# First units of an attention and mixer kernel: scores, state products and k transposes in the PSUM banks of token mixing, first state read from PSUM, order planned anew

## The chip, the core and the metric

The kernel runs on one core of a Trainium2 chip. The metric is the device time of one execution in microseconds (us); three executions of the kernel before took 617.54, 617.64 and 617.73. Engines are named as in the profile: PE (TensorE; PEld its weight loads), DVE (VectorE), ACT (ScalarE), POOL (GpSimd, here mostly a queue of transfers) and SP (SyncE, the other queue of transfers).

## What is computed

Four batches of 768 tokens, 8 heads of 48 (so 384 channels). A gated linear attention, then a mixer with complex phases over tokens and a channel product, then a gated unit with a second product over tokens:

```python
for t in range(S):
    state = alpha[:, :, t, :, None] * state + einsum('bhd,bhe->bhde', k[:, :, t], v[:, :, t])
    y[:, :, t] = einsum('bhd,bhde->bhe', q[:, :, t], state)
x = y as (B, S, 384)

theta = x @ w_theta
u = x + einsum('ts,bsd->btd', w_tok_r, x * cos(theta)) + einsum('ts,bsd->btd', w_tok_i, x * sin(theta))
x = u + maximum(u @ w_ch, 0)

h = maximum(x @ w_in, 0);  u, v = h[..., :512], h[..., 512:]
v_n = (v - mean(v)) / sqrt(var(v) + 1e-6)
v_s = einsum('ts,bsd->btd', w_spatial, v_n) + b_spatial[None, :, None]
out = (u * v_s) @ w_out
```

## The kernel before

Each batch is cut into six units of 128 tokens, 24 units u in all, each of two halves c of 64 tokens. A unit's path: its decay `al`, its `qk` and its `vd` are loaded by SP (`load_al`, `load_qk`, `load_v`). DVE scans the decay (`att_scan`, L485 to L489: a scan, a small reciprocal, a scan) and multiplies q and k with it (`att_qk`, L497). PE makes scores (`att_a`, L511, in the text also A), which DVE masks (`att_mask`, L519; one half is then moved to other partitions by SP, `move_a`), transposes k (`att_k`, L535, K), which ACT copies to `kt` (L539), and makes the state products `psu` of the two halves (`att_u`, L551, U). On DVE `att_t` (L566, L568) adds the decayed state to a product, into `tmp`, and `att_s` (L560) multiplies `tmp` with a decay into `ss`, the state that the next half reads. `att_y` (L585, Y) makes the unit's outputs `psy` from `ss`, q, masked scores and v; ACT copies them to `x` (L593). PE transposes x (`tr_p`, L605, P); ACT takes from it the upper part `xh` (`tr_h`, L609) and `xT`, DVE the rest (`tr_l`, L627). `th_p` (L637 with six matmuls, L640 with three, H) is the product with w_theta; ACT and DVE make r, sine and cosine and `z` from it (L644 to L666), and ACT and DVE split `z` in two parts `zs` (`z_h`, `z_l`, L670, L674). `tokmix(u, m, ri)` (L697, T) adds a unit's part of token mixing, six pieces of six matmuls a unit, into five PSUM banks acc0 to acc4 that stay with a batch until `evac`. Piece m = 0 writes acc0 and acc1, m = 1 acc1 and acc2, m = 2 acc3 and acc4; acc1 is zeroed ahead by DVE. After a batch, `ch_h` and `ch_l` split the result and `ch_p` (L739) multiplies it with w_ch into `psc`, which DVE adds (`ch_e`, L749). The second mixer (L812 to L920) follows for all batches.

PSUM has eight banks: five for acc, and three (`ps_tile`, tag `ps`) that all other results share: a `psa` for scores takes two of them, `psu` two, `psy` two, `psk`, `pst`, `th`, `psc` one each.

The weights come as 64-bit numbers in chunks, `raw`, by POOL's queue in two buffers. ACT takes part of a chunk into `zeros` (`top`, L382), DVE joins both into `wf` (`join`, L388), after which the buffer can be loaded again; ACT writes the upper part (`high`, L400) and DVE the lower (`low`, L408). The chunks are numbered: 0 and 1 w_theta (1 half as large), 2 to 13 the token weights of unit s and part ri (2 + 2s + ri; `in_w_tr` and `in_w_ti`), 14 and 15 w_ch.

The order of all steps on all engines is fixed when the program is built. Each step has an engine, an estimated cost, its predecessors and the buffers it needs; `latest` works out due times backwards, the tables OFF, OFF0, OFF3, UNIT and PIECE shift them per kind of step, batch, unit and chunk, and `order` plays the steps through in time and emits whichever is due first on an engine that is free. Each engine then works its steps strictly in that order, and so do the queues of SP and POOL.

Of the kernel before, what the change touches and what calls it, by code (L numbers as in the profile page):

```python
# [23 lines left out]
MAGIC = 12582912.0  # L24
# [26 lines left out]
    "cp": -158.47, "ce": 100.03, "cd": 447.07, "raw": -618.18, "bits": -49.65, "sgn": 1376.56, "mag": -710.85,  # L51
    "mul": 267.54, "high": -1464.25, "low": -859.94, "v": 16.07, "vr": 273.38, "vb": 866.6, "vw": 1642.18,
    "vm": -337.76, "vh": -1658.38, "vl": -557.55, "g_u": -7.44, "g_r": -485.14, "g_s": -429.06, "g_m": 441.16,
    "g_h": -488.08, "g_l": -904.44, "o_p": 15.51, "o_e": -843.47, "x2h": -1179.65, "x2l": 281.95, "x2": -552.71,
# [17 lines left out]
}  # L72
OFF3 = {
# [21 lines left out]
SSB = 6  # L95
# [6 lines left out]
ISSUE = {"dma": 0.4, "queue": 0.55}  # L102
AHEAD = {"dma": 0.8, "queue": 1.1}


# [180 lines left out]
def attention_mixer_kernel(  # L286
# [902 lines left out]
```

## Time and profile before

| | |
|---|---|
| median of three executions | 617.64 us |
| profiled execution, its own time | 613.52 us |
| its span, first to last instruction | 611.8 us |
| PE busy | 576.1 us, 94% |
| DVE busy | 399.2 us, 65% |
| ACT busy | 243.5 us, 40% |
| POOL busy | 24.8 us, 4% |

The profile is that of one execution. Busy time is the time in which at least one instruction of an engine runs. In a row of the trace the time in brackets is how long the engine stood idle before it, and for whom. The page cuts the span in forty slices of 15.3 us.

### The profile page before, as it was taken

The page shows a single profiled execution, that of the slowest core. Times are in us where ns is not written, and L with a number is a line of the kernel's source. Part 1 is how long each engine was busy: PE and PEld are TensorE (multiplying, and loading weights), DVE is VectorE, ACT ScalarE, POOL GpSimd, SP SyncE. Part 2 cuts the span into 40 slices and gives each one's busy share as a digit, 9 for nine tenths or more (in the row PEclk, how much of TensorE's full clock was granted, in tenths as well). Part 3 has the DMA queues.
Part 4 walks back from the last instruction along what each step waited for, and adds up shares of the span by engine and source line. Part 5 has one row for each costly group of instructions (what it writes and reads, how often), then busy time and mean ns, then how long its engine had stood idle before and what let it go on. Part 6 is the DMA issues. An engine that isn't in the chain of part 4 may idle for free.

```text
span 611.8 us, 13444 instructions
## 1 busy us (share of the span) xinstructions
PE 576.1 (94%) x5803; PEld 524.2 (86%) x5803; DVE 399.2 (65%) x671; ACT 243.5 (40%) x445; POOL 24.8 (4%) x45
## 2 busy tenths in 40 slices
PE   0688999999999999999999999999999999999997
PEld 0566878888888888888899889999999999999997
DVE  6898997986789796679855696544346434553060
ACT  2575665432534354233643543324233322242032
POOL 1101100000000000000000011000000000000000
PEclk9998999999999999999999999999999999999999
DMA  8667576333342423324023662200100010001002
GB/s 333 199 221 267 181 253 208 112 111 105 124 145 82 158 88 120 118 76 124 15 87 130 220 219 78 77 1 27 39 14 2 26 40 14 0 14 40 13 14 77
DMA packets 27370, 63.77 MB, mean 104 GB/s; under 512 B 2992, under 2 KB 12720, under 8 KB 26800
## 3 DMA queue, kind: packets, MB, share of 16 engines
q1 hardware_dynamic: 25136, 51.13, 24.9%
q0 software_dynamic: 2176, 11.80, 5.5%
q8 instruction: 45, 0.74, 0.5%
q14 instruction: 13, 0.11, 0.0%
HBM read 50.33 MB, written 9.44 MB: 98 GB/s over the span
## 4 chain that ended last, share of the span: by engine, by line
PE 73%; DVE 8%; DMA 4%; issue 2%; ACT 0%; SPq 0%; POOL 0%; DVEq 0%; ACTq 0%
PE acc L697 17%; PE sp L881 16%; PE po L910 8%; PE pu L865 8%; PE psv L823 8%; PE psc L739 4%; DMA al<-in_al 3%; PE th L637 3%; PE psy L585 3%; PE psu L551 1%; DVE al L485 1%; PE th L640 1%; PE psa L511 1%; DVE xT L711 1%; PE psk L535 1%
## 5 line engine op out<-in xcount | busy, mean ns | idle before, releaser
L697 PE MATMUL acc<-w,zs 128*128 128x512 f32 (+1 forms) x864 | 177.6, 347 | 0.3
L697 PEld LDWEIGHTS acc<-w,zs 128*128 128x128 f32 x864 | 134.8, 189 | 17.9 <-DVE zs L674 0.5
L881 PE MATMUL sp<-w,vns 128*128 128x384 f32 x576 | 105.6, 335 | 0.0
L881 PEld LDWEIGHTS sp<-w,vns 128*128 128x128 f32 x576 | 100.9, 188 | 0.7
L865 PE MATMUL pu<-xs,w 128*128 128x384 f32 x288 | 55.1, 336 | 0.0
L823 PE MATMUL psv<-w,xs 128*128 128x512 f32 x216 | 54.1, 395 | 0.0
L910 PE MATMUL po<-w,gs 128*128 128x384 f32 x288 | 53.2, 335 | 0.0
L865 PEld LDWEIGHTS pu<-xs,w 128*128 128x128 f32 x288 | 50.4, 188 | 0.8
L910 PEld LDWEIGHTS po<-w,gs 128*128 128x128 f32 x288 | 50.4, 188 | 0.5
L890 DVE TENSOR_TENSOR t<-sp,bsb 128x384 f32<-128x384 f32 x32 | 17.8, 557 | 50.7 <-PE sp L881 49.8
L823 PEld LDWEIGHTS psv<-w,xs 128*128 128x128 f32 x216 | 40.1, 187 | 7.8
L897 ACT CAST gs<-t 128x384 fp32r<-128x384 f32 x32 | 16.1, 514 | 74.4 <-DVE t L891 74.4
L739 PE MATMUL psc<-us,wch 128*128 128x384 f32 (+1 forms) x243 | 41.4, 321 | 1.7 <-DVE xT L749 1.1
L739 PEld LDWEIGHTS psc<-us,wch 128*128 128x128 f32 x243 | 37.8, 189 | 2.6 <-DVE xT L749 1.3
L901 DVE TENSOR_TENSOR gs<-t,gs 128x384 fp32r<-128x384 f32 x32 | 17.6, 556 | 30.8 <-ACT gs L897 30.7
L485 DVE TENSOR_TENSOR_SCAN al<-al,heads 112x536 f32<-112x536 f32 x24 | 30.5, 1271 | 7.9 <-DMA al<-in_al 7.8
L843 POOL TENSOR_TENSOR rs<-rs,mhalf 128x1 f32<-128x1 f32 x24 | 14.8, 618 | 460.7 <-DMA x<-x2d 275.1
L637 PE MATMUL th<-wth,xh 128*128 128x384 f32 x144 | 31.2, 352 | 1.7 <-DVE ax L519 1.0
L644 ACT ACTIVATE kk<-th,magic 128x384 f32<-128x384 f32 x24 | 13.9, 578 | 44.5 <-PE th L640 44.5
L489 DVE TENSOR_TENSOR_SCAN al<-al,heads 112x536 f32<-112x536 f32 x24 | 30.6, 1275 | 0.8
L535 PE MATMUL psk<-cst_sb,qk 112*128 112x112 f32 x96 | 14.0, 274 | 17.6 <-DVE qk L497 16.0
L497 DVE TENSOR_TENSOR qk<-qk,al 112x1024 f32<-112x1024 f32 x24 | 29.2, 1219 | 0.9 <-DMA qk<-in_qk 0.8
(77 smaller groups left out, 799.2 us busy)
## 6 DMA issues: line engine op xcount, KB each, us to landing
qk<-in_qk SPq DMA_DIRECT2D x24, 512.0 KB, 4.6
vd<-in_v SPq DMA_DIRECT2D x24, 288.0 KB, 4.1
al<-in_al SPq DMA_DIRECT2D x24, 268.0 KB, 2.7
raw<-in_w_ti POOLq DMA_DIRECT2D x6, 768.0 KB, 4.8
raw<-in_w_tr POOLq DMA_DIRECT2D x6, 768.0 KB, 5.9
x<-x2d SPq DMA_DIRECT2D x4, 1152.0 KB, 5.0
out<-o SPq DMA_DIRECT2D x24, 192.0 KB, 1.9
x2d<-xT SPq DMA_DIRECT2D x6, 576.0 KB, 3.3
```

Of the source, the lines that this page charges most:

```text
L485: nc.vector.tensor_tensor_scan(out=back[:, ::-1], data0=line[:, ::-1], data1=one[:, ::-1], initial=1.0, op0=ALU.mult, op1=ALU.add)
L489: nc.vector.tensor_tensor_scan(out=line, data0=line, data1=one, initial=0.0, op0=ALU.mult, op1=ALU.add)
L497: nc.vector.tensor_tensor(out=x, in0=x, in1=st[u]["ar"], op=ALU.mult)
L535: nc.tensor.transpose(psk[:, a, :], kh[:, a].rearrange("p c s -> p (c s)"), ident[:112, :112])
L585: nc.tensor.matmul(psy[par][64 * c:64 * c + 64, a, :], w, v, start=part == 0 or first, stop=part == 1,)
L637: nc.tensor.matmul(th, xh[:, 0, k], wth[:, pr, k], start=(k == 0 and pr == 0), stop=False)
L697: nc.tensor.matmul(acc[b, n][:, c0:c1], zs[:, pl, ri, m * 128:(m + 1) * 128], w[:, pr, t0:t1], start=first and n != 1, stop=last, skip_gro ...
L739: nc.tensor.matmul(ps, wch[:, pl, k, m * 128:(m + 1) * 128], us[:, pr, k], start=(n == 0), stop=(n == 3 * KD - 1),)
L823: nc.tensor.matmul(ps, xs2[:, pl, k, o:o + 128], win[pr, "v"][:, k], start=(n == 0), stop=(n == 3 * KD - 1),)
L865: nc.tensor.matmul(pu, win[f // 2][:, pl, k * 256 + f % 2 * 128:k * 256 + f % 2 * 128 + 128], xq[b, h][:, pr, k], start=(n == 0), stop=(n ...
L881: nc.tensor.matmul(sp[:, :TH], vns[b, s][:, pl, f * 128:(f + 1) * 128], wsp[s][:, pr, t], start=(n == 0), stop=(n == 3 * NS - 1),)
L910: nc.tensor.matmul(po, gs[b][:, pl, f, s * 128:(s + 1) * 128], wo[f // 2][:, pr, f % 2 * DM:(f % 2 + 1) * DM], start=(n == 0), stop=(n == ...
```

## The change

The function `unit_ps` gives the first EARLY units a bank of token mixing in place of a shared one: scores (`psa`) acc0 and acc2, state products (`psu`) acc3 and acc4, the k transpose (`psk`) acc3, for units 0 to 2. Outputs, x transposes and `th` stay with the three shared banks.

In the first unit of a batch, the first state product is no longer copied to `tmp`: `att_s(u, 1)` reads `psu` itself. (`att_i`, a matmul that would add a state in PSUM, and `th_n`, `th_m`, with which `r` would be made by PE, come into the text, but STP and THP are empty and `att_i` is for other units, so neither issues an instruction.) One more constant, `unmagic`, is set by DVE at the start. The ring of `ss` has five buffers instead of six.

The planner's costs of transfers are set a little higher, its engines start at times FIRST instead of 0, and all five tables have new numbers, so that the order differs throughout the program.

```diff
+EARLY = {'a': 3, 'u': 3, 'y': 0, 'k': 3, 't': 0, 'h': 0}
+BANKS = {'a': [0, 2], 'u': [3, 4], 'k': [3]}
+THP = ()
+STP = ()
-SSB = 6
+SSB = 5
-ISSUE = {"dma": 0.4, "queue": 0.55}
-AHEAD = {"dma": 0.8, "queue": 1.1}
+FIRST = {"pe": 0.8, "dve": 1.6, "act": 2.2, "pool": 1.5, "dma": 0.74, "none": 0.0, "queue": 1.5}
+ISSUE = {"dma": 0.44, "queue": 0.57}
+AHEAD = {"dma": 0.8, "queue": 1.0}
 PIECE = {
-    "0": -331.5, "1": -441.59, "2": -706.09, "3": -715.22, "4": -65.4, "5": -167.4, "6": 8.34, "7": 308.88,
+    "0": -679.06, "1": -1253.41, "2": -607.1, "3": -578.67, "4": -112.62, "5": -191.42, "6": 185.74, "7": -410.35,
...
+    def unit_ps(u, what, n, shape, name):
+        if u < EARLY[what]:
+            bank = f"acc{BANKS[what][n]}"
+            size = math.prod(shape[1:])
+            t = accp.tile([128, 512], F32, tag=bank, name=bank)[:, :size]
...
+        return ps_tile(shape, name)
...
-            st[u]["psa", e] = ps_tile([128, 2, 2, 64], "psa")
+            st[u]["psa", e] = unit_ps(u, "a", e, [128, 2, 2, 64], "psa")
-        psk = st[u]["psk"] = ps_tile([128, NP, 112], "psk")
+        psk = st[u]["psk"] = unit_ps(u, "k", 0, [128, NP, 112], "psk")
-            st[u]["psu", c] = ps_tile([128, NP, D], "psu")
+            st[u]["psu", c] = unit_ps(u, "u", c, [128, NP, D], "psu")
...
-        nc.vector.tensor_tensor(out=ss, in0=tmps.pop(0), in1=decay(u, c), op=ALU.mult)
+        tmp = st[u]["psu", 0][:112] if c and summed(u) else tmps.pop(0)
+        nc.vector.tensor_tensor(out=ss, in0=tmp, in1=decay(u, c), op=ALU.mult)
+
+    def summed(u):
+        return u % NS == 0 or u in STP
...
-        psu = st[u]["psu", c][:112]
-        if u % NS == 0 and c == 0:
-            nc.vector.tensor_copy(out=tmp, in_=psu)
-        else:
-            nc.vector.tensor_tensor(out=tmp, in0=psu, in1=st[u]["ss", c], op=ALU.add)
+        nc.vector.tensor_tensor(out=tmp, in0=st[u]["psu", c][:112], in1=st[u]["ss", c], op=ALU.add)
```

What the new tables do to the order is seen in the program's rows. Three places follow, with row by row what an engine does; line numbers of the new program are some 20 to 35 higher.

The first is DVE's start. `al` is the decay of a unit (101 is unit 0's; 105 before and 103 now are unit 1's), `wf` the joined chunk, `qk` the decayed q and k. Before:

```order
L485 SCALAR_TENSOR_TENSOR al_101<-al_101,heads_89 112x536
L488 RECIPROCAL al_101<-al_101 112x8
L489 SCALAR_TENSOR_TENSOR al_101<-al_101,heads_89 112x536
L388 SCALAR_TENSOR_TENSOR wf_122<-raw_103,zeros_92 128x768
L485 SCALAR_TENSOR_TENSOR al_105<-al_105,heads_89 112x536
L488 RECIPROCAL al_105<-al_105 112x8
L489 SCALAR_TENSOR_TENSOR al_105<-al_105,heads_89 112x536
L408 SCALAR_TENSOR_TENSOR w_127<-wf_122,w_127 128x768
L497 TENSOR_TENSOR qk_109<-qk_109,al_101 112x1024
```

And now:

```order
L506 SCALAR_TENSOR_TENSOR al_101<-al_101,heads_91 112x536
L509 RECIPROCAL al_101<-al_101 112x8
L510 SCALAR_TENSOR_TENSOR al_101<-al_101,heads_91 112x536
L506 SCALAR_TENSOR_TENSOR al_103<-al_103,heads_91 112x536
L509 RECIPROCAL al_103<-al_103 112x8
L510 SCALAR_TENSOR_TENSOR al_103<-al_103,heads_91 112x536
L409 SCALAR_TENSOR_TENSOR wf_129<-raw_105,zeros_94 128x768
L518 TENSOR_TENSOR qk_114<-qk_114,al_101 112x1024
L429 SCALAR_TENSOR_TENSOR w_131<-wf_129,w_131 128x768
```

The scan of unit 1 moved ahead of the first chunk's `join`, and the first `att_qk` ahead of its `low`.

The second is ACT's start, from its second chunk on: `zeros` is the taking of a chunk, `w` and `wth` its `high`, then `kt`, `x`, `xh` and `xT` of units 0 and 1. Before (from the third `zeros` on):

```order
L382 ACTIVATE zeros<-raw 128x768
L539 COPY kt<-psk 128x448
L400 ACTIVATE w<-wf 128x768
L382 ACTIVATE zeros<-raw 128x384
L400 ACTIVATE wth<-wf 128x384
L539 COPY kt<-psk 128x448
L382 ACTIVATE zeros<-raw 128x768
L400 ACTIVATE wth<-wf 128x768
L382 ACTIVATE zeros<-raw 128x768
L593 COPY x<-psy 128x4x48 x2
L609 CAST xh<-pst 128x384
```

And now (from the second `zeros` on):

```order
L403 ACTIVATE zeros<-raw 128x384
L560 COPY kt<-acc_138 128x448
L421 ACTIVATE wth<-wf 128x384
L403 ACTIVATE zeros<-raw 128x768
L560 COPY kt<-acc_219 128x448
L421 ACTIVATE wth<-wf 128x768
L403 ACTIVATE zeros<-raw 128x768
L620 COPY x<-psy 128x4x48 x2
L421 ACTIVATE w<-wf 128x768
L403 ACTIVATE zeros<-raw 128x768
L636 CAST xh<-pst 128x384
```

The chunks of w_theta moved to the second and third place, `xh` of unit 0 now stands behind the fifth `zeros` (before, the sixth), with one `high` and one `zeros` between `x` and `xh`. POOL's queue loads in the same order of chunks: 13, 1, 0, 2, 3, 7 now, 13, 3, 2, 1, 0, 10 before. SP loads `al`, `al`, `vd`, `cst`, `qk` now, and loaded `al`, `al`, `qk`, `cst`, `qk`, `vd` before.

The third is DVE ahead of the first token mixing: `r` of unit 1 (L648, now L681), masks of unit 2, `qk` of units 2 and 3, `z` and `zs` of unit 0. Before:

```order
L497 TENSOR_TENSOR qk_314<-qk_314,al_266 112x1024
L497 TENSOR_TENSOR qk_378<-qk_378,al_307 112x1024
L666 TENSOR_TENSOR z_413<-z_413,x_316 128x768
L648 SCALAR_TENSOR_TENSOR r_450<-kk_427,th_405 128x384
L519 TENSOR_TENSOR ax_454<-psa_432,cst_sb_69 128x256
L519 TENSOR_TENSOR am_461<-psa_433,cst_sb_69 128x256
L388 SCALAR_TENSOR_TENSOR wf_467<-raw_275,zeros_92 128x768
L674 TENSOR_TENSOR zs_452<-z_413,zs_452 128x768
```

And now:

```order
L540 TENSOR_TENSOR ax_430<-acc0_397,cst_sb_69 128x256
L540 TENSOR_TENSOR am_432<-acc2_398,cst_sb_69 128x256
L506 SCALAR_TENSOR_TENSOR al_311<-al_311,heads_91 112x536
L509 RECIPROCAL al_311<-al_311 112x8
L510 SCALAR_TENSOR_TENSOR al_311<-al_311,heads_91 112x536
L681 SCALAR_TENSOR_TENSOR r_465<-kk_463,th_420 128x384
L518 TENSOR_TENSOR qk_366<-qk_366,al_311 112x1024
L700 TENSOR_TENSOR z_428<-z_428,x_291 128x768
L409 SCALAR_TENSOR_TENSOR wf_475<-raw_298,zeros_94 128x768
L595 TENSOR_TENSOR tmp_497<-acc3_441,ss_372 112x192
L708 TENSOR_TENSOR zs_495<-z_428,zs_495 128x768
```

The scan of unit 3 and `r` of unit 1 moved ahead of `att_qk(3)` and of unit 0's `z` and `zs`, and a state sum of unit 2 stands there too. On PE the steps up to the first token mixing were K0 A0 K1 A1 U0 U1 Y0 P0 Y1 H0 P1 H1 K2 A2 K3 A3 and are now K0 A0 U0 A1 K1 U1 Y0 P0 Y1 H0 P1 K2 A2, the first part of H1, U2, its second part, K3 A3; Y2 now stands behind the first piece, U3 behind the third.

## Rows read from the trace of the kernel before

**Rows 1.** Page, the span in forty slices: PE's busy tenths.

```profile
PE   0688999999999999999999999999999999999997
```

**Rows 2.** Windows: length, busy PE, PEld, DVE, ACT, POOL (instructions), granted clock, DMA.

```profile
3.44:85.98 82.54, 57.94 (x871) 48.70 (x872) 72.11 (x108) 45.42 (x76) 7.88 (x14) 0.98 0.71 248
15.63:80.74 65.11, 53.71 (x849) 45.01 (x850) 58.52 (x90) 41.14 (x70) 7.34 (x13) 0.97 0.67 228
...
30.00:40.00 10.00, 8.71 (x92) 7.43 (x92) 9.86 (x14) 6.77 (x14) 0.53 (x1) 1.00 0.92 326
...
50.00:60.00 10.00, 8.26 (x177) 6.82 (x181) 8.51 (x14) 6.10 (x10) 1.07 (x2) 0.83 0.74 252
80.74:340.00 259.26, 256.02 (x3482) 224.12 (x3477) 201.77 (x320) 111.71 (x216) 0.00 (x0) 1.00 0.36 118
```

**Rows 3.** Waits (us, times, longest): PE up to 61 us; DVE, 3.4 to 86.

```profile
PE psk L535 <- DVE qk L497: 16.0, 2, 15.6
PE psu L551 <- ACT kt L539: 3.0, 2, 2.3
...
PE psu L551 <- DVE ax L519: 1.4, 1, 1.4
PE psk L535 <- ACT kt L539: 1.1, 1, 1.1
...
DVE wf L388 <- ACT zeros L382: 5.8, 3, 3.6
...
DVE w L408 <- ACT w L400: 0.9, 1, 0.9
...
DVE wth L408 <- ACT wth L400: 0.6, 1, 0.6
```

**Rows 4.** Timeline of DVE from its first scan: start, duration, [idle before].

```profile
3.44 1.27 DVE L485 TENSOR_TENSOR_SCAN al<-al,heads 112x536 f32<-112x536 f32 x1 [1.08 <-DMA al<-in_al]
...
4.98 1.27 DVE L489 TENSOR_TENSOR_SCAN al<-al,heads 112x536 f32<-112x536 f32 x1
9.90 0.96 DVE L388 SCALAR_TENSOR_TENSOR wf<-raw,zeros 128x768 uint32<-128x768 uint32 x1 [3.64 <-ACT zeros L382]
...
14.36 1.22 DVE L497 TENSOR_TENSOR qk<-qk,al 112x1024 f32<-112x1024 f32 x1
```

**Rows 5.** DVE's groups, shapes apart: busy us, mean ns, idle before.

```profile
L560 DVE TENSOR_TENSOR ss<-tmp,al 112x192 f32<-112x192 f32 x44 | 15.6, 355 | 1.0
...
L566 DVE COPY tmp<-psu 112x192 f32<-112x192 f32 x4 | 1.4, 351 | 2.6 <-PE psu L551 2.6
```

**Rows 6.** Issues, us to landing: at 1.6-2.0 us, at 2.1-2.2, all (median).

```profile
qk<-in_qk SPq DMA_DIRECT2D x1, 512.0 KB, 6.8
...
raw<-in_w_ti POOLq DMA_DIRECT2D x1, 768.0 KB, 8.8
...
al<-in_al SPq DMA_DIRECT2D x24, 268.0 KB, 2.7
...
raw<-in_w_tr POOLq DMA_DIRECT2D x6, 768.0 KB, 5.9
```

**Rows 7.** Timeline of PE, single rows between 30 and 85 us.

```profile
32.98 2.29 PE L637 MATMUL th<-wth,xh 128*128 128x384 f32 x6
...
37.27 1.33 PE L637 MATMUL th<-wth,xh 128*128 128x384 f32 x6 [0.69 <-ACT xh L609]
...
43.26 1.74 PE L697 MATMUL acc<-w,zs 128*128 128x256 f32 x6
...
80.74 1.31 PE L697 MATMUL acc<-w,zs 128*128 128x256 f32 x6
...
83.06 1.28 PE L637 MATMUL th<-wth,xh 128*128 128x384 f32 x6 [1.01 <-DVE ax L519]
```

**Rows 8.** Timeline of DVE, the state product `att_s(5, 1)`.

```profile
85.63 0.35 DVE L560 TENSOR_TENSOR ss<-tmp,al 112x192 f32<-112x192 f32 x1
```

**Rows 9.** Waits of PE from 80.74 us to the end, the longest.

```profile
PE pst L605 <- DVE xT L749: 1.3, 1, 1.3
```

More of the change, by code (lines that the diff above doesn't have):

```diff
@@ L44 @@
 OFF = {
[6 rows of a table removed]
[L51 to L54, printed above, removed]
[6 rows of a table added]
+    "ce": -880.9, "cd": 1489.21, "raw": -473.63, "bits": -921.27, "sgn": 2210.86, "mag": 1308.55, "mul": 394.64,
+    "high": -1533.93, "low": -1460.32, "v": 143.66, "vr": -33.61, "vb": 570.25, "vw": 3214.81, "vm": 824.68,
+    "vh": -1464.39, "vl": 159.16, "g_u": 130.27, "g_r": -797.41, "g_s": -2037.89, "g_m": -595.78, "g_h": -2481.78,
+    "g_l": -415.04, "o_p": -583.54, "o_e": 982.08, "x2h": -1502.64, "x2l": 734.13, "x2": -883.6,
 }
@@ L167, in finish @@
                 push(when[f], "ready", f)
+    for e, t in free.items():
+        push(t, "tick", None)
     for k in keys:
@@ L312, in ps_tile @@
         return psp.tile(shape, F32, tag="ps", name=name)
+    def unit_ps(u, what, n, shape, name):
[3 more added lines that the diff above has]
+            t = accp.tile([128, 512], F32, tag=bank, name=bank)[:, :size]
+            if len(shape) == 2:
+                return t
+            sub = {f"d{i}": k for i, k in enumerate(shape[1:])}
+            return t.rearrange(f"p ({' '.join(sub)}) -> p {' '.join(sub)}", **sub)
+        return ps_tile(shape, name)
     cst_sb = const.tile([128, 192], F32, name="cst_sb")
@@ L318, in attention_mixer_kernel @@
     nc.vector.memset(magic, MAGIC)
+    unmagic = const.tile([128, 1], F32, name="unmagic")
+    nc.vector.memset(unmagic, -MAGIC)
     halfpi = const.tile([128, 1], F32, name="halfpi")
@@ L331, in attention_mixer_kernel @@
     minus = pb.tile([128, 128], F32R, name="minus") if XLP else None
+    negative = pb.tile([128, 128], F32, name="negative") if THP else None
     NB = 2
@@ L426, in conv @@
             c["queue"] = nc.gpsimd if n < NQ else nc.sync
-            k = step(early + OFF["raw"], "queue" if n < NQ else "dma", 2.1 * size, raw_f64, n, after=before, tiles=[raw])
+            k = step(early + OFF["raw"], "queue" if n < NQ else "dma", 2.2 * size, raw_f64, n, after=before, tiles=[raw])
             k = step(early + OFF["mag"], "act", cost(0.54, 0.86), top, n, after=[k], tiles=[raw, zero])
@@ L559, in att_s, with att_i @@
         ss = st[u]["ss", c] = pa.tile([112, NP, D], F32, tag="ss", name="ss", bufs=SSB)
[L560 removed]
+        tmp = st[u]["psu", 0][:112] if c and summed(u) else tmps.pop(0)
+        nc.vector.tensor_tensor(out=ss, in0=tmp, in1=decay(u, c), op=ALU.mult)
+    def summed(u):
+        return u % NS == 0 or u in STP
+    def att_i(u):
+        nc.tensor.matmul(
+            st[u]["psu", 0][:112].rearrange("p a e -> p (a e)"), ident[:112, :112],
+            st[u]["ss", 0].rearrange("p a e -> p (a e)"), start=False, stop=True, skip_group_check=True,
+        )
     def att_t(u, c):
         tmp = tmps[0] = pa.tile([112, NP, D], F32, tag="tmp", name="tmp", bufs=1)
[L564 to L568 removed]
+        nc.vector.tensor_tensor(out=tmp, in0=st[u]["psu", c][:112], in1=st[u]["ss", c], op=ALU.add)
     def att_y(u):
         qh, vd = st[u]["qh"], st[u]["vd"]
[L572 removed]
+        psy = st[u]["psy"] = [unit_ps(u, "y", n, [128, NP, D], "psy") for n in range(2)]
         for a in range(NP):
@@ L644, in th_k, with th_n, th_m @@
         nc.scalar.activation(kk, st[u]["th"], AF.Identity, bias=magic)
+    def th_n(u):
+        nc.scalar.activation(st[u]["kk"], st[u]["kk"], AF.Identity, bias=unmagic)
+    def th_m(u):
+        nc.tensor.matmul(st[u]["th"], negative, st[u]["kk"], start=False, stop=True, skip_group_check=True)
     def th_r(u):
@@ L661, in th_s @@
         else:
[L662 removed]
+            r, turn = (st[u]["th"], TURN) if u in THP else (st[u]["r"], -TURN)
+            nc.scalar.activation(z[:, 1], r, AF.Sin, scale=turn)
     def z_m(u):
@@ L926, in negate @@
     def negate():
-        nc.scalar.activation(minus, ident, AF.Identity, scale=-1.0)
+        for x in (minus, negative):
+            if x is not None:
+                nc.scalar.activation(x, ident, AF.Identity, scale=-1.0)
     step(0.0, "dma", 0.32, load_cst)
-    if XLP:
-        step(0.0, "act", 0.3, negate, after=[("load_cst",)])
+    if XLP or THP:
+        step(0.0, "act", 0.5, negate, after=[("load_cst",)])
     conv_small(w_theta, wth, "wth", scale=INV_2PI)
@@ L952, in attention_mixer_kernel, with ps @@
         xt = ("xT", 2, b)
-        def ps(*n):
-            return ("ps", 3, (u,) + n)
+        def ps(what, n=0):
+            if u < EARLY[what]:
+                return (f"acc{BANKS[what][n]}", 1, (u, what, n))
+            return ("ps", 3, (u, what, n))
         def at(name, eng, cost, fn, *args, after=(), tiles=(), by=None):
@@ L986, in attention_mixer_kernel @@
             if ss:
-                k = at(f"s{c}", "dve*", 0.27, att_s, c, after=[ksc, ktx], tiles=[al, *ss, *tmps_in])
+                k = at(f"s{c}", "dve" if c and mine else "dve*", 0.27, att_s, c, after=[ksc, ktx], tiles=[al, *ss, *tmps_in])
                 kss.append(k)
-            if not (final and c):
+            if c == 0 and mine:
+                ktx = at("t0", "pe", 0.33, att_i, after=[k, ku, ("load_cst",)], tiles=[ps("u", 0), *ss]) if i else ku
+            elif not (final and c):
                 ktx = at(f"t{c}", "dve", 0.27, att_t, c, after=[k, ku], tiles=[ps("u", c), ("tmp", 1, (u, c)), *ss])
```

33 lines of the change are left out of this document (18 added, 15 removed), and 35 rows, old and new, of tables (OFF, OFF0, OFF3).

## Prediction, made before the changed kernel ran

> **What bounds the kernel now.** I read the page's slices first: PE is full from the eighth of the forty slices on and not ahead of it [rows 1]. So there are two stretches. Cut up by windows, PE has 53.71 us of work in the 65.11 us from its first matmul at 15.63 to 80.74, and 256.02 in the 259.26 us from there to 340 [rows 2]. What can be won lies before about 80 us: 15.6 us in which PE has nothing yet, and 11.4 us (65.11 less 53.71) of holes behind that. Later, the longest single wait is 1.3 us [rows 9].
>
> The waits of PE up to 61 us name what the change is about [rows 3]. 15.6 us are for the first decayed k (`qk` from DVE). Of the holes two are PSUM: a k transpose that waits until ACT has read the one before (1.1), state products that wait until DVE has masked scores (1.4); these want buffers, not data. Others want data: `psu` waits for the transposed k (3.0, two waits, the longer 2.3).
>
> But who paces these 80 us? From its first scan at 3.44 up to the end of `att_s(5, 1)`, DVE works 72.11 of 82.54 us [rows 2, 8]. Whatever order PE has, it needs these DVE steps; so I count what the new order does to DVE's 10.4 us of idling, and then what PE makes of it.
>
> **The change part by part.** *Banks.* Units 0 to 2 take scores, state products and k transposes from the five accumulator banks, idle until token mixing starts. PE's work is the same instructions. It takes away the buffer waits above: 1.1 + 1.4 = 2.5 us of PE holes. On the path that sets the end it is worth nothing of its own as long as DVE (87% busy) is what PE catches up with; what it does is to let PE run its early work as soon as DVE has it. Where DVE is not the pace, these 2.5 us are the bound above. The banks add a wait: the first tokmix pieces of unit 0, at 43.26 in before [rows 7], must now follow unit 2's masks and state sums on DVE, since m = 2 writes acc3 and acc4; behind a waiting piece stand all of PE's later steps. DVE does these steps for the states of unit 2 anyway, so the price stays inside the DVE budget below.
>
> *First state.* The COPY of `psu` to `tmp` goes, four in all, 0.35 each [rows 5]; the decay multiply reads PSUM instead. One of the four lies in the paced stretch: -0.3 us. The other three stand where PE is full: 0. The bound from the other side is a multiply that is slower from PSUM; the COPY, which reads PSUM, and the multiply, which read SBUF, cost the same for the same shape (351 and 355 ns) [rows 5], so 0.
>
> *Order at the start.* Unit 1's scan now stands directly behind unit 0's, ahead of the first weight chunk (`wf`, `join`). In before DVE had nothing from 6.25 to 9.90: 3.64 us until ACT's `zeros` of that chunk [rows 4]. A scan step takes 3.44 to 6.25, 2.81 us, and fits, if the second `al` is there: both are the first that SP issues, and an `al` lands in 2.7 [rows 6]. So 0.83 us of the hole are left: **2.8 us won**. The first `att_qk` then follows the chunk, at 10.8 in place of 14.36, if `qk` has landed. In before it landed 6.8 us behind its issue at 1.7, so at 8.5 [rows 6]. Now `vd` and `cst` (288 + 96 KB) go ahead of it on SP, but POOL's second chunk is 384 KB instead of 768: two `al`, `qk`, two chunks before, or two `al`, `vd`, `cst`, `qk` and a chunk and a half now, are 2584 KB in either order. In before these had all landed when POOL's second chunk had, 8.8 us behind an issue that ran at 2.1 to 2.2: by 11.0 [rows 6]. So `qk` is there at 11.0 at the latest, `att_qk` takes 1.22 [rows 4], and PE's first matmul comes at about 12.2, 3.4 us earlier.
>
> *Order of chunks.* DVE waits 5.8 us in three waits for ACT's `zeros`, the longest 3.6: the other two make 2.2, or 1.1 each. It waits 0.9 and 0.6 us in `low` for ACT's `high` [rows 3]. The new order puts `att_qk`, masks or state steps between `join` and `low` of the first chunks, so I take these 1.5 as gone. Of the 2.2 I take half, 1.1: the chunks come earlier in the program, but one lands 5.9 us behind its issue [rows 6] and only two are in flight, as before; the bounds are 0 and 2.2. *New waits.* On ACT the cast `xh` of unit 0 stands behind the `zeros` of the fifth chunk (second place above), and POOL issues that chunk only when the third, the big one of theta, has been joined; in before it was the sixth, but PE was later still. Behind the cast wait `tr_l(0)` on DVE and `th_p(0, 0)` on PE. I take for it what a wait for such a chunk costs on the mean, -1.1; 0 if the chunk is early, 3.6, the longest of the three, if not. Unit 5's scan now stands close behind `att_s(3, 1)`, which frees its `al` buffer: 2.7 to land [rows 6], beside a `join` and a `low` of 0.9 each, as long as the `wf` of [rows 4]: -0.9. A third, of `r` of unit 1 for PE, is a rival below.
>
> *Sum.* 2.8 + 0.3 + 1.5 + 1.1 - 1.1 - 0.9 = 3.7 us less idling of DVE. PE has 27 us to give until 80.74 (15.6 and 11.4), so I take its gain as what DVE gives. To this comes one PE wait of that stretch that did not hang on DVE's pace but on order: 1.0 us at 83.06, where `th` wanted the PSUM buffer of scores that DVE had not masked yet [rows 7]. It had one tokmix piece between the scores of unit 5 and itself, now it has three; each lasts 1.3 [rows 7]. It goes: 0.8 to 1.0. Together **4.5 us**. The profiled execution took 613.5 (span 611.8 and 1.7 around it), so it would be 609.0; the median of the shown runs is 4.1 above that execution, and I take the saved time as the same there: 617.6 - 4.5 = 613.1. Behind 80 us the order changes everywhere too; the waits of PE there are few and none is longer than 1.3 [rows 9], so +-1.3 for one of them gone or come; with the chunk waits' bounds (+1.1, -1.1) this makes the forecast's own range 611.4 to 615.0.
>
> **The rivals.** *All holes go.* If both new waits vanish and the chunk waits too, DVE gains 2.8 + 0.3 + 1.5 + 2.2 = 6.8, with PE's 1.0 7.8; and a piece of PE's low clock may go as well: from 50 to 60 us, behind the wait of 2.3 us, the granted clock is 0.83 [rows 2, 3]. 8 us: 609.6. For it: PE gets its inputs in time for nearly all of unit 0 to 2. Against: it leaves DVE 3.6 of 10.4 us idle, 96% busy for 80 us.
>
> *The clock stays down.* Six `th` matmuls took 2.29 us at 32.98 and 1.33 at 37.27 [rows 7]. [...] In the new order (third place above) `r` of unit 1 stands on DVE ahead of `att_qk(3)`, `z_m(0)` and the `zs` that the first tokmix piece needs, and on PE U2 now stands between the two parts of `th_p(1)`, whose end `r` waits for. At the slow durations the first part is 1.0 longer, the second, with half the matmuls, 0.5, and for U2 I take 0.7, an estimate by its smaller matmuls: 2.2 us in which DVE waits. 4.5 - 2.2 = 2.3: 615.3.
>
> [...]
>
> *The banks decide nothing.* The change could do less than it says: if chunks arrive no earlier than before, DVE's steps behind them stay where they were, the head start ends as longer waits for `zeros` and `xh` (3.6, the longest seen [rows 3], in place of 1.1: 2.5 more), nothing of the 1.1 is won and 0.9 of the 1.5 in `low` comes back: 4.5 - 2.5 - 1.1 - 0.9 = 0: 617.6. For it: three of DVE's waits hang on chunks. Against: POOL issues a chunk when DVE has joined one, and DVE joins earlier.
>
> *Slower.* The pieces `psc` (ch_p) of the channel product (6 for each of three batches) now stand among other K, P and Y of the next batch than before, with three shared PSUM buffers, emptied by DVE. One such wait costs 1.3 us, at 236 us [rows 9]. It decides from the fifth of the eighteen on that waits so (5 x 1.3 = 6.5, against 4.5). Two in each of the three batches: 7.8 - 4.5, so 620.9. Against it: DVE has 22% idle from 80 to 340 [rows 2].
>
> **How the numbers follow.** Forecast 613.1: 0.55. All holes 609.6: 0.15. Clock 615.3: 0.14. Nothing 617.6: 0.09. Slower: 0.07. Two tenths of a per cent, 1.2 us, is about what a measurement can tell from no change: faster means under 616.4. Forecast, all holes and nearly all of the clock case lie there: 0.83; same 0.10; slower 0.07. The range has to hold 0.8: forecast, clock and most of the case of all holes, so from 609.0 to 616.4; what it leaves out are the last two cases and the tails.
>
> **What would show it.** First matmul at 12.2 (11.5 to 13); no 3.6 us hole on DVE before 10; no PSUM buffer wait of PE among units 0 to 2; `psk` and `psu` not behind ACT or masks; a wait of DVE `xh` of about 1 us near 26; first tokmix piece ahead of 43.26 by 3 us (by 1 if the clock stays down); DVE idle from its first scan to `att_s(5, 1)` of about 6.7 us, not 10.4; no wait of `th` for masks near 80. Wrong if the first matmul is early and unit 3's first tokmix piece, at 80.74 in before, is not, or if more than 2 us of new PE waits stand between 80 and 340.

## The result, and the profile after

The changed kernel took 609.96 us (median of four executions, 609.87 to 611.83) beside 617.59 for the kernel before (615.29 to 617.73): a ratio of 0.9892, 95% interval 0.9863 to 0.9922. The predicted 613.1 was 3.1 too high; the time lies inside the range of 609.0 to 616.4, near its lower end. Faster was the sign that came.

The profiled execution of the changed kernel took 610.03 us (span 608.3), that of the kernel before 613.52. So the two profiles differ by 3.5 us, and the medians by 7.6. Both numbers are needed below. One further execution of the changed kernel, in the last comparison, took 3131.63 us; its time is left out everywhere.

The page's slices of PE, to lay beside [rows 1]: in both kernels PE is full (9, that is 90% or more) from the fifth slice on. The four slices ahead of it read 1, 7, 7, 8 now and 0, 6, 8, 8 before.

```profile
PE   1778999999999999999999999999999999999997
```

To see where the 3.5 us lie, I cut both executions at the first `psv` of the second mixer, which is the same instruction in both and has the same 1451 matmuls behind it. Windows of the kernel before, and then of the changed one (length, busy PE, PEld, DVE, ACT, POOL with instructions, granted clock, DMA share, GB/s):

```profile
0.00:86.00 86.00, 57.96 (x872) 48.70 (x873) 73.34 (x114) 46.93 (x78) 10.00 (x21) 0.98 0.70 244
86.00:345.25 259.25, 257.02 (x3485) 225.00 (x3483) 197.94 (x312) 113.20 (x217) 0.00 (x0) 1.00 0.37 120
...
345.25:611.80 266.55, 261.14 (x1451) 250.53 (x1449) 127.96 (x246) 83.32 (x151) 14.82 (x24) 1.00 0.13 44
```

```profile
0.00:86.00 86.00, 63.47 (x993) 52.89 (x997) 74.94 (x118) 47.18 (x83) 9.50 (x20) 0.96 0.71 241
86.00:341.35 255.35, 252.37 (x3376) 221.03 (x3368) 197.98 (x309) 114.01 (x214) 0.53 (x1) 1.00 0.40 128
...
341.35:608.30 266.95, 262.90 (x1451) 252.33 (x1449) 124.38 (x243) 81.54 (x149) 15.11 (x24) 1.00 0.11 39
```

The first `psv` comes 3.9 us earlier (345.25 to 341.35). Up to there PE idles 25.5 us (341.35 less 63.47 and 252.37) in place of 30.3 (345.25 less 57.96 and 257.02): 4.8 us less, of which its matmuls, 0.9 us longer in sum, take some back. Behind it the changed kernel is 0.4 us longer: 1.4 us less idle, and 1.8 us more for the same 1451 matmuls.

Of the 4.8 us, 3.2 are the earlier first matmul (15.63 in before [rows 2], 12.43 now). Timelines of the changed kernel's start, on DVE and then on PE (start, duration, [idle before <- whom it waited for]); DVE's answer to [rows 4]:

```profile
4.99 1.27 DVE L510 TENSOR_TENSOR_SCAN al<-al,heads 112x536 f32<-112x536 f32 x1
6.18 1.25 DVE L506 TENSOR_TENSOR_SCAN al<-al,heads 112x536 f32<-112x536 f32 x1
...
10.05 0.96 DVE L409 SCALAR_TENSOR_TENSOR wf<-raw,zeros 128x768 uint32<-128x768 uint32 x1 [1.07 <-ACT zeros L403]
11.14 1.23 DVE L518 TENSOR_TENSOR qk<-qk,al 112x1024 f32<-112x1024 f32 x1
...
15.91 0.35 DVE L582 TENSOR_TENSOR ss<-acc,al 112x192 f32<-112x192 f32 x1
```

```profile
12.43 1.01 PE L556 MATMUL acc<-cst_sb,qk 112*128 112x112 f32 x4 [12.43 <-DVE qk L518]
```

The second scan fills the hole of 3.64 us, and 1.07 of it is left. The row at 15.91 is the multiply that now reads the state product in PSUM. The waits, to lay beside [rows 3]: PE up to 86 us (behind the one for the first `qk`), then DVE from 3.4 to 86.

```profile
...
PE psk L556 <- DVE qk L518: 3.2, 1, 3.2
PE pst L632 <- ACT x L620: 2.3, 2, 1.7
PE psy L612 <- DMA ay<-ax: 1.3, 1, 1.3
PE th L664 <- ACT x L620: 0.9, 1, 0.9
PE acc L572 <- ACT kt L560: 0.7, 1, 0.7
PE psk L556 <- DVE ax L540: 0.5, 1, 0.5
...
```

```profile
DVE al L506 <- DMA al<-in_al: 2.0, 2, 1.1
DVE wf L409 <- ACT zeros L403: 1.9, 2, 1.1
DVE xh L654 <- ACT xT L641: 1.5, 2, 1.3
DVE qk L518 <- DMA qk<-in_qk: 1.3, 1, 1.3
DVE wth L429 <- ACT wth L421: 0.9, 1, 0.9
DVE r L681 <- ACT kk L671: 0.9, 1, 0.9
DVE w L429 <- ACT w L421: 0.4, 1, 0.4
```

PE no longer waits for ACT's read of an earlier k transpose; one wait of 0.5 us for masks is left, at 81.13 us (`psk` of a later unit, one of the shared buffers). Both waits for chunks (`wf`) are shorter. The forecast's new wait for `xh` is there.

### The profile page after: what moved, and what is told of

Read it like the earlier page. It is cut to its first block, busy times and chain, and to the rows that moved or that the text cites. A ratio compares the mean times of both kernels' runs of the same rounds, so it can differ in the third digit from the quotient of the medians.

```text
span 608.3 us, 13440 instructions
## 1 busy us (share of the span) xinstructions
PE 578.7 (95%) x5803; PEld 526.3 (87%) x5803; DVE 397.3 (65%) x668; ACT 242.7 (40%) x445; POOL 25.1 (4%) x45
## 4 chain that ended last, share of the span: by engine, by line
PE 75%; DVE 10%; DMA 8%; issue 4%; ACT 2%; SPq 1%; DVEq 0%; ACTq 0%; POOLq 0%
PE acc L731 17%; PE sp L915 17%; PE psv L857 8%; PE pu L899 8%; PE po L944 8%; PE psc L773 6%; DMA qk<-in_qk 4%; PE psy L612 3%; PE th L664 3%; PE th L667 1%; DVE qk L518 1%; PE psu L572 1%; DMA al<-in_al 1%; PE psa L532 1%; DVE wf L409 1%
## 5 line engine op out<-in xcount | busy, mean ns | idle before, releaser
L731 PE MATMUL acc<-w,zs 128*128 128x512 f32 (+1 forms) x864 | 174.1, 347 | 1.5 <-DVE xT L745 0.8
L915 PE MATMUL sp<-w,vns 128*128 128x384 f32 x576 | 106.9, 338 | 0.0
L870 DVE BATCH_NORM_STATS2 stt<-v 128x6 f32<-128x512 f32 x24 | 16.6, 690 | 21.4 <-ACT v L865 21.2
L704 ACT CAST zs<-z 128x768 fp32r<-128x768 f32 x24 | 20.0, 834 | 24.0 <-DVE z L700 13.1
```

Of the source, the lines that this page charges most:

```text
L704: nc.scalar.copy(out=st[u]["zs"][:, 0], in_=st[u]["z"])
L731: nc.tensor.matmul(acc[b, n][:, c0:c1], zs[:, pl, ri, m * 128:(m + 1) * 128], w[:, pr, t0:t1], start=first and n != 1, stop=last, skip_gro ...
L915: nc.tensor.matmul(sp[:, :TH], vns[b, s][:, pl, f * 128:(f + 1) * 128], wsp[s][:, pr, t], start=(n == 0), stop=(n == 3 * NS - 1),)
```

## Experiments

In the expectations, theory A says that DVE paces the first 80 us, B that the banks themselves give the gain, C that the granted clock decides it; D to F are told where they come up. Executions of one kernel scatter by several us (the kernel before from 614.22 to 619.92 on one chip), so I compare means with the mean of the kernel before in the same comparison. The changed kernel itself came out 6.0 us under it twice (`e0_new_again`, `e12_new_third`, ratios 0.9903, interval 0.9871 to 0.9935, and 0.9902, interval 0.9880 to 0.9925); that is the yardstick. In the traces I again use the first `psv` as the mark; each trace is of one execution, and such a one can lie anywhere in the scatter.

| run | what it is | mean, less before (us) | ratio to before (95%) |
|---|---|---|---|
| e1_old_order_banks | before, banks for A and U | -0.4 | 0.9994 (0.9972 to 1.0016) |
| e2_new_order_shared | changed, no banks | -5.0 | 0.9925 (0.9897 to 0.9953) |
| e3_scan_late | changed, scan and first `att_qk` late again | -2.0 | 0.9965 (0.9938 to 0.9992) |
| e5_old_scan_early | before, scan and first `att_qk` early | -2.2 | 0.9961 (0.9938 to 0.9985) |
| e4_more_dve | changed, 5.6 us more DVE work | -1.2 | 0.9974 (0.9949 to 0.9999) |
| e6_xh_first | changed, `xh` of unit 0 sooner | -6.4 | 0.9887 (0.9851 to 0.9923) |
| e7_keep_warm | changed, PE kept busy near 37 us | -5.8 | 0.9896 (0.9863 to 0.9930) |
| e8_late_filler | changed, 1.7 us of DVE work at 348 us | -5.7 | 0.9908 (0.9879 to 0.9937) |
| e9_less_dve | changed, six subtractions off DVE, six products on PE and six copies on ACT instead | -2.2 | 0.9965 (0.9949 to 0.9982) |
| e11_both | e9 and e6 together | -2.6 | 0.9962 (0.9942 to 0.9982) |

**The yardstick**, the changed kernel without an edit.

> The new kernel unchanged, as the yardstick of the next three. All theories: 610.0 within 0.5. What it is to settle beside that: the kernel before took 613.5 in its profiled execution and 617.6 in three others. If the gain is the 3.5 us between the two profiled executions, before stays near 613.5 here; if it is 7.6, before is near 617.6 in nearly all executions and its profiled one was an exception.

> The changed kernel once more, as the yardstick of this call: about 1.0 to 1.1% under the kernel before, as in the earlier calls (609.7 beside 616.3).

Measured: -6.0 both times.

**Banks or order?** First the old order with the banks, then the new order without them.

> The order of before, word for word, but scores and state products of units 0 to 2 in the banks of token mixing (not the k transposes: in this order they would lock acc3 against the state products). Theory A, DVE paces the first 80 us and the banks only permit another order: the PE wait for masks before the state products (1.4 us) goes, the end moves by less than 1 us against before. Theory B, the waits for shared PSUM buffers were themselves the loss: 2.5 us less than before.

```diff
+EARLY = {"a": 3, "u": 3}
+BANKS = {"a": [0, 2], "u": [3, 4]}
...
-            st[u]["psa", e] = ps_tile([128, 2, 2, 64], "psa")
+            st[u]["psa", e] = unit_ps(u, "a", e, [128, 2, 2, 64], "psa")
...
-            st[u]["psu", c] = ps_tile([128, NP, D], "psu")
+            st[u]["psu", c] = unit_ps(u, "u", c, [128, NP, D], "psu")
```

> The order of the new kernel, word for word, with all results in the three shared PSUM buffers again. Theory A: the masks and state steps on DVE now come later because PE waits for buffers in an order made for more of them: 1 to 2.5 us more than the new kernel, 611 to 612.5, and DVE's idle time up to 86 us grows by as much. Theory B: the whole gain hangs on the banks, at least 4 us more, 614 or above. If the order alone is what counts: no more than 0.5 us above the new kernel.

```diff
-        if u < EARLY[what]:
+        if False and u < EARLY[what]:
```

Measured: -0.4 (within 0.2% of before) and -5.0. PE's waits of the old order with banks, up to 61 us:

```profile
PE acc L562 <- ACT kt L550: 3.4, 1, 3.4
PE pst L616 <- ACT x L604: 3.3, 1, 3.3
PE psu L562 <- ACT kt L550: 2.9, 1, 2.9
```

The wait for masks is gone, and what PE waits for next, the data, takes its place. So theory B falls: banks alone give nothing that can be measured, and most of the gain comes with the order. On top of the new order the banks are worth 1 us by the means, which the scatter of six executions each doesn't tell from nothing. The k transposes were not among the banks of the first of the two runs. No run takes out the state product read from PSUM, the shorter ring of `ss` or the planner's new costs by themselves.

**The start.** The early scan undone in the changed kernel (put behind the first `join`, that of chunk 13), and done alone in the kernel before (put ahead of it). Each time the first `att_qk` goes with it, behind or ahead of the first `low`.

> The new kernel, but on DVE the scan of unit 1 stands behind the join of the first chunk again and the first att_qk behind its low, as before. Theory A, each us that DVE idles at the start is paid at the end: the 2.6 us hole ahead of the first join is back, first matmul near 15.9 and 2.5 us more than the new kernel, 612.5. Rival, the loads of the weight chunks pace the start and the hole was free: first matmul near 15.9 as well, but at most 0.7 us at the end, 610.7.

```diff
+MOVES = ((("att_scan", 1), ("join", 13)), (("att_qk", 0), ("low", 13)), (("att_qk", 1), ("att_qk", 0)))
```

> The kernel before, with one thing of the new order alone: on DVE unit 1's scan ahead of the first chunk's join, and the first att_qk ahead of its low. First matmul near 12.2 in place of 15.6. Theory A: DVE's 2.8 us are given on to the end, 2 to 3 us less than before, 613.5 to 614.5 beside 616.3. Rival, in the old order of chunks (token weights ahead of w_theta) the theta chunks hold th of unit 0, so the head start ends in a longer wait there: less than 0.7 us.

```diff
+MOVES = ((("att_scan", 1), ("join", 13)), (("att_qk", 0), ("low", 13)))
```

Measured: 4.0 us worse than the yardstick, and 2.2 better than before. DVE with the scan undone:

```profile
5.31 1.27 DVE L511 TENSOR_TENSOR_SCAN al<-al,heads 112x536 f32<-112x536 f32 x1
10.50 0.96 DVE L410 SCALAR_TENSOR_TENSOR wf<-raw,zeros 128x768 uint32<-128x768 uint32 x1 [3.92 <-ACT zeros L404]
```

The hole is back, and the first matmul comes at 16.23 us; in the old order with the early scan it comes at 12.38. A start worth 2.2 to 4.0 us bears out the term of 2.8 in size, and it is between a third and two thirds of the gain of 6.0. Neither figure is the start alone. With the scan undone, PE's matmuls up to the first `psv` (350.13) also take 320.1 us in place of 315.8, at granted clocks of 0.50 to 0.75 from 20 to 60 us, while PE idles 30.0 us in place of 25.5. And in the old order with the early scan PE stands for buffers that the masks hold:

```profile
PE th L638 <- DVE ax L520: 2.7, 1, 2.7
...
PE psk L536 <- DVE ax L520: 2.2, 1, 2.2
...
PE psu L552 <- DVE ax L520: 1.7, 1, 1.7
```

These were 1.0 us (`th`), nothing and 1.4 in the kernel before. So once the data comes early, the shared buffers do hold PE up; the old order with both the early scan and the banks wasn't run.

**DVE as the pace.** More work on DVE (eight statistics of 0.7 us on data that nobody waits for, within units 2 to 5), a wait of DVE taken away (`xh` and `xT` of unit 0 ahead of ACT's part of weight chunk 3, `top`; where the expectation of e11 speaks of a row of scores, it is this chunk that is meant), and less work on DVE.

> The new kernel with two idle DVE instructions more behind each att_qk of units 2 to 5 (their results are used by nothing), about 0.65 us each, so 5.2 us of DVE work between 30 and 78 us. Theory A, DVE paces the first 80 us: 3.5 to 5 us more than the new kernel, 613 to 615. Rival, PE or the chunk loads pace it and DVE has room (it idles about 7 us there): less than 1.5 us more.

```diff
+        if 2 <= u < 6:
+            for n in range(2):
+                idle = pa.tile([112, 6], F32, tag="idle", name="idle", bufs=1)
+                nc.vector.bn_stats(out=idle, in_=st[u]["qk"][:, n * 512:(n + 1) * 512])
```

> The new kernel, but on ACT xh and xT of unit 0 stand ahead of the fifth chunk's zeros instead of behind it. Theory A: the wait of DVE for xh (1.3 us at 26.9) and 1 us of PE's wait for th go; since DVE is the pace, 1 us less than the new kernel, about 608.7. Rival, the next waits (r, qk of unit 3) take it: within 0.4.

```diff
+MOVES = ((("tr_h", 0), ("top", 3)), (("tr_t", 0), ("top", 3)))
```

> The changed kernel with the low part of xT of all six units made by a TensorE product with a negated identity and an ACT copy, and not by a VectorE subtraction (0.47 us each, 2.8 us off VectorE before 86 us; the order is otherwise as it was). Theory A, VectorE paces the units: 1.5 to 2.8 us less than the changed kernel. Theory F, the chain between the engines paces them and VectorE's work there is only along the way: the longer path to the low part (TensorE, then ACT) costs as much as it gives, within 0.7 us or longer.

```diff
+XL = (0, 1, 2, 3, 4, 5)
...
-        if u in XLP:
+        if u in XL:
+            tr_x(u)
             nc.scalar.copy(out=xh[:, 1], in_=st[u]["pst"])
             return
```

> The same as the run before it, and the high and low part of the first unit's xT ahead of the fourth row of scores on every queue, so that VectorE does not wait for `xh` near 26 us (1.3 us). Theory A: 2.0 to 3.5 us less than the changed kernel. Theory F: within 1 us of it.

In e9 and e11 the low part of xT is not the one that the computation needs, so their times are read as those of the same instructions and no more. Measured: 4.8 us lost by the added work (5.6 us by the profile, where one takes 694 ns); 0.4 won by the wait taken away, within the scatter (in its trace the wait for `xh` is gone, and those for `qk` are 1.9 us in place of 1.3); and 3.8 (e9) and 3.5 (e11) *lost* by the work taken away. Theory A had 1.5 to 2.8 won.

The added work cost in two ways. In its trace PE idles 29.9 us up to the first `psv` (349.76) in place of 25.5, and its matmuls take 319.9 us in place of 315.8, with a granted clock of 0.90 from 3.44 to 85.98 us in place of 0.96. So about half of what that execution lost is waiting (4.4 us), and half is matmuls that took 4.1 us longer at that clock. DVE's timeline with less work, e9, then the same place in the changed kernel:

```profile
27.90 0.35 DVE L584 TENSOR_TENSOR ss<-tmp,al 112x192 f32<-112x192 f32 x1
30.89 1.23 DVE L520 TENSOR_TENSOR qk<-qk,al 112x1024 f32<-112x1024 f32 x1 [2.64 <-DMA qk<-in_qk]
```

```profile
29.37 0.35 DVE L582 TENSOR_TENSOR ss<-tmp,al 112x192 f32<-112x192 f32 x1
29.64 1.22 DVE L518 TENSOR_TENSOR qk<-qk,al 112x1024 f32<-112x1024 f32 x1
```

DVE is 1.5 us earlier, and then stands for a load. SP issued that load at 23.69 (at 23.30 in the changed kernel, where it was there in time), and the DMA engines are 95 and 96% busy from 24 to 32 us in the two. Later in e9 the product that replaces the subtraction makes a longer path, PE, ACT, PE, at unit 2. ACT and PE there:

```profile
52.87 0.48 ACT L655 CAST xh<-pst 128x384 fp32r<-128x384 f32 x1 [2.23 <-PE pst L646]
...
58.04 0.58 ACT L674 ACTIVATE kk<-th,magic 128x384 f32<-128x384 f32 x1 [2.98 <-PE th L670]
```

```profile
52.31 0.52 PE L646 MATMUL pst<-xh,minus 128*128 128x384 f32 x1
53.40 2.29 PE L667 MATMUL th<-wth,xh 128*128 128x384 f32 x6 [0.57 <-ACT xh L655]
```

So for work added theory A comes true. For work taken away it doesn't: DVE's lead ends at a load. But the edit doesn't measure less DVE work by itself, since it also puts six products on PE (2.6 us in sum) and six copies on ACT. Up to the first `psv` (345.87) PE of e9 idles 26.5 us in place of 25.5, and its matmuls take 319.4 in place of 315.8; from 50 to 60 us the granted clock of that execution was 0.66, beside 0.91 in the changed kernel. What the load, the longer path, the products and the clock each cost of the 3.8 us wasn't separated, so theory F isn't shown either.

**The clock.** Sixteen matmuls that nobody reads, behind the second part of `th_p(1)`.

> The new kernel with sixteen matmuls of no use (w_theta times itself into acc0) on PE behind the second th of unit 1, in the 3.2 us in which PE waits for qk of unit 3. They keep PE working there. Theory C, the low clock behind that wait is what the first token mixing pays: its pieces at 40 and 49 us take 1.2 instead of 2.1 to 2.3 us, and the end comes 1.5 to 2.5 us earlier, 607.5 to 608.5. Theory A: the pieces get faster but PE then waits longer for zs and weights from DVE near 68; at most 0.6 us at the end.

```diff
+    def warm():
+        t = accp.tile([128, 512], F32, tag="acc0", name="acc0")[:, :DM]
+        for n in range(16):
+            nc.tensor.matmul(t, wth[:, 0, 0, :128], wth[:, 0, 1], start=True, stop=True)
```

Measured: -5.8, no gain over the yardstick. Windows of the changed kernel, then of this one (columns as above):

```profile
30.00:40.00 10.00, 6.84 (x118) 5.24 (x116) 9.71 (x15) 6.52 (x13) 0.53 (x1) 0.91 0.43 142
40.00:50.00 10.00, 7.84 (x123) 6.43 (x120) 9.05 (x16) 6.67 (x12) 1.06 (x2) 0.84 0.80 259
50.00:60.00 10.00, 10.00 (x141) 8.77 (x140) 8.59 (x14) 6.75 (x13) 1.06 (x2) 0.91 0.50 157
```

```profile
30.00:40.00 10.00, 8.47 (x133) 6.96 (x132) 9.88 (x15) 6.16 (x12) 0.00 (x0) 1.00 0.43 137
40.00:50.00 10.00, 7.42 (x124) 5.79 (x125) 9.46 (x16) 6.70 (x12) 1.06 (x2) 1.00 0.81 258
50.00:60.00 10.00, 8.95 (x139) 7.64 (x138) 8.60 (x14) 7.18 (x13) 1.06 (x2) 1.00 0.58 187
```

The clock reads 1.00 in all three stretches, PE is done sooner with its pieces (the first six matmuls take 1.6 us in two parts in place of 2.05) and waits instead (0.9 us ahead of 42.8 in place of 0.5): the first `psv` comes at 342.66, not ahead of the changed kernel's 341.35. By the interval alone a gain of 1.5 us would still be possible; the trace shows none. So theory C, that the clock decides the time of the changed kernel, has nothing for it here. It doesn't follow that the clock is free: with the scan undone, and with more work on DVE, matmuls that took 4.3 and 4.1 us longer, at granted clocks of 0.81 and 0.90 from 3.44 to 85.98 us, are part of what was lost. No kernel tried here beats the changed one by more than the scatter.

**The end of token mixing.** Comparing the traces I saw that 1.7 us of PE's waits at `psc` near 350 us are gone, because the low part of the x2 load (`xs`, 1.35 us on DVE) no longer stands ahead of `ch_l`. The next kernel puts some DVE work back there (four statistics of 0.43 us, 1.7 in sum).

> The changed kernel with four short statistics on VectorE (some 1.4 us together, on data that nothing waits for) right ahead of the first low part of the last batch's channel mixing. Theory D, the end of token mixing gave some 1.7 us that the prediction did not count, because 1.35 us of VectorE no longer stands ahead of that low part: PE waits for `us` return (0.6 us or more at psc) and the time is 1.0 to 1.7 us longer than the changed kernel. Theory E, the place had slack either way and the gain is all at the start: no PE wait for `us` over 0.3 us, and within 0.5 us of the changed kernel.

```diff
+        if (b, h) == (B - 1, 0):
+            for k in range(4):
+                nc.vector.bn_stats(out=idle, in_=xT[b][:, k % KD, :w])
```

Measured: -5.7, 0.4 us worse than the yardstick on the mean and 0.8 better on the median; the scatter doesn't tell D from E. The trace does: PE at that place in this kernel, and in the changed one.

```profile
348.49 0.39 PE L777 MATMUL psc<-us,wch 128*128 128x256 f32 x2
350.61 11.23 PE L777 MATMUL psc<-us,wch 128*128 128x256 f32 x79 [1.73 <-DVE us L765]
```

```profile
345.55 10.11 PE L773 MATMUL psc<-us,wch 128*128 128x256 f32 x81
```

The wait is back as D says, at 1.73 us, and the `psc` matmuls take 1.5 us more (11.6 in all). They go with a lower clock: from 350 to 355 us the granted clock is 0.70, where it is 1.00 in the changed kernel (0.97 beside 1.00 from the first `psv` to 400 us), and of the `psc` matmuls behind the wait those that start from 352 to 355 us mostly take 415 ns, those ahead of and behind them mostly 283 (310 on the mean of all 81, beside 284). Here PE has no slack, and the wait costs nearly twice its length (3.2 us for 1.73). And yet from its first `psv` at 344.30 to the end it is only 1.55 us longer than the changed kernel (268.50 beside 266.95), because other matmuls of the same count are 1.9 us shorter, as they were in the kernel before. Groups of `sp` and `po`, busy us and mean ns, in before, changed, and e8:

```profile
L881 PE MATMUL sp<-w,vns 128*128 128x384 f32 x576 | 105.6, 335 | 0.0
...
L910 PE MATMUL po<-w,gs 128*128 128x384 f32 x288 | 53.2, 335 | 0.0
```

```profile
L915 PE MATMUL sp<-w,vns 128*128 128x384 f32 x576 | 106.9, 338 | 0.0
...
L944 PE MATMUL po<-w,gs 128*128 128x384 f32 x288 | 53.8, 338 | 0.4 <-ACT v L865 0.4
```

```profile
L919 PE MATMUL sp<-w,vns 128*128 128x384 f32 x576 | 105.5, 336 | 0.0
...
L948 PE MATMUL po<-w,gs 128*128 128x384 f32 x288 | 53.2, 336 | 0.4 <-ACT v L869 0.4
```

So the changed kernel gives back in slower `sp` and `po` what it wins at `psc`, and its late stretch comes out at +0.4 us.

## Why the prediction was right, and where it was off

*Right.* DVE's first hole filled, 3.64 us down to 1.07 (2.6 won, forecast 2.8); the first matmul at 12.43 (12.2); the multiply that reads PSUM at the price of one that doesn't (0.35 us at 15.91, the first of its kind; up to 86 us 351 ns beside a mean of 353); the waits for chunks (5.8 less 1.9 is 3.9, of which 2.6 is the first hole, so 1.3 against 1.1); a new wait for `xh` of 1.28 near 26.9 (1.1); one for `al` of 0.88 at 46.73 (0.9), though at unit 4's scan and in place of two (0.38 and 0.70) that the sum didn't see go; no wait of `th` for masks near 80, though 0.5 us of `psk` for masks at 81.13 took half of that 1.0 back; first token mixing piece at 40.01 in place of 43.26, 3.3 earlier (3). The banks by themselves are worth nothing that can be measured while data is what PE lacks, as the part on them says and as the old order with banks shows (-0.4 us). Between 80.74 and 340 us PE idles 3.4 us in place of 3.2, so the rival of waits at the channel product had no part. PE's idle time up to the first `psv` fell by 4.8 us, where the sum had 4.5.

*Right total, partly wrong sum.* That the totals agree (4.8 and 4.5) is in part luck. The step "I take its gain as what DVE gives" put 3.7 of the 4.5 us on DVE's idling up to `att_s(5, 1)`. That fell by 1.65 only: from 10.4 to 8.8. Window up to the end of that step (columns as above):

```profile
3.44:80.27 76.83, 58.23 (x895) 48.95 (x896) 68.05 (x102) 41.29 (x71) 6.83 (x12) 0.96 0.72 246
```

Mis-sized was the term of `low`: "I take these 1.5 as gone", and 1.3 of it stayed (`wth` 0.9, `w` 0.4). New waits that had no term came beside it: `r` for ACT 0.9, and 1.3 for `qk` in place of 0.8. And the 0.3 for the COPY is work that goes, not idling. What PE won over and above came from order and not from idling: `att_s(5, 1)` itself comes at 79.92 in place of 85.63, with 68.05 us of DVE work ahead of it and not 72.11. The sum looked at how long DVE idles ahead of a step, and left out which work is ahead of it. The run with the order but no banks (-5.0) against the scan alone (-2.2), on another chip, puts what the order gives beyond the early scan at some 2.7 us; which of its many moves give them wasn't tried. The reading of [rows 1] was wrong too (full from the fifth slice, not the eighth); no term hangs on it, since the stretch up to 80.74 us was read from windows.

*The miss of 3.1 us.* "The median of the shown runs is 4.1 above that execution, and I take the saved time as the same there." This step failed. For the profiled execution it forecast 609.0, and 610.03 came. But the changed kernel's median is where its profiled execution is (609.96 and 610.03; again 609.73 and 609.01), while 613.52 is nearly the lowest time of the kernel before among all that were taken: of 68 executions on three chips behind the table only the lowest, 613.35, is under it. The offset belonged to one unusually fast execution, not to the program. What that execution had that others of the same kernel lack can't be read, since none of them has a trace; that stays open. The nearest trace is that of the old order with banks, whose times don't differ from those of the kernel before; it is of an ordinary execution (615.66, with a mean of 616.1). Up to its first `psv` (347.39) PE idles 33.3 us, not 30.3, and 1.0 of the 3.0 is there at the first matmul (16.59, not 15.63), behind a first weight chunk that ACT took up 1.0 later. If such executions are the rule, the sum was made from a profile that lacked some of the idling that the new order takes away.

The 7.6 us between the medians are those of four executions a side; both later comparisons have 6.0 between the means, 1.5 more than the sum's 4.5. The forecast's own range, 611.4 to 615.0, was missed. That the wider range holds the time is owed to the case of all holes at its lower end, so it is luck as far as the mechanism goes.

*The rivals.* The clock's rival came true only in part, and not where it was put: unit 1's six `th` matmuls took 1.32 us at 32.29, the shorter of the two durations in [rows 7]. Its 2.2 us were the author's estimate from these durations; that the longer one means a lower clock is not shown: unit 0's six took 2.29 us at 27.14 in the changed kernel, and the granted clock reads 1.00 from 27.1 to 29.5 us, as it does for the long ones of before (1.00 from 32.98 to 35.20). A lower granted clock came later, 0.91, 0.84 and 0.91 in the three stretches from 30 to 60 us: 0.56 from 38 to 40 us, behind PE's wait of 3.2 us, 0.68 from 48 to 49.3, behind one of 1.7, and 0.50 from 49.34 to 51.60, where six matmuls of token mixing took 2.29 us. In the changed kernel this cost nothing that the runs can show, since with the clock at 1.00 from 30 to 60 us (e7) PE waited. The time of 609.6 that the case of all holes gave is near the measured one, but not its mechanism: 8.8 us of DVE's idling are left, not 3.6.

*"Wrong if"* named unit 3's first token mixing piece, at 80.74 in before: it came at 81.50, later, so by its own sign the forecast was wrong. That mark was badly chosen, since the new order puts more of PE's work ahead of it (58.97 us, 900 instructions, in place of 53.71, 849). A mark has to have the same work ahead of it in both orders, as the first `psv` nearly has.

## What to carry to other kernels

Before a sum is made against a profiled execution, look where that execution lies among the times of the same kernel: an offset to the median is a property of an execution, not of the program. When an order is planned anew, cut both traces at an instruction with the same work behind it, and split each side into idle and busy time of the bounding engine; a step's time alone says little. Before buffers are added, look whether the data is already there: with the old start they gave nothing that could be measured (-0.4 us), and with the early scan alone PE stood for them (2.7, 2.2 and 1.7 us). Moving work off the busiest engine onto others may only uncover the transfer that lies close behind it (a wait of 2.64 us for `qk` in e9), while adding work to it cost nearly its full length here (4.8 of 5.6 us), in part because PE's matmuls took 4.1 us longer, at a granted clock of 0.90 in place of 0.96.

## What was not expected of the hardware

- The same 864 matmuls `sp` and `po` took 338 ns each in the changed kernel and 335 in the kernel before, at a granted clock of 1.00 in both, some 1.9 us in sum. It goes with the kernel and not with the execution: 105.6 us for `sp` in all three profiles of the old order, 106.9 in nine of the new order, and 105.5 in e8, whose one difference in storage is a small tile among the constants (e4 has a tile as small in the pool of the units, and 106.9). What sets it is not shown: the storage differs (the change has a buffer of `ss` less and a constant more, too), but so does the wait of 1.73 us that only e8 has at `psc`; neither was tried alone.
- Executions of one kernel scatter by some 6 us on one chip (614.22 to 619.92 for the kernel before), and the granted clock differs between them too (0.972 to 0.994 on the mean of the span in the twelve with the scan undone). With the scan undone, the profiled execution had 0.71, 0.50, 0.67 and 0.75 in the four stretches from 20 to 60 us, 0.972 on the mean of its span, and was the slowest of its twelve, at 618.77. The clock doesn't explain all of the scatter: another of the twelve took 618.71 at 0.991.
- A wait of 1.73 us at a place where PE had no slack (e8, near 350 us) was followed by a granted clock of 0.70 from 350 to 355 us, and cost 1.5 us more in slower matmuls. Waits of 0.61 and 1.08 us at the same place in the kernel before left the clock at 1.00.
